# Seven block products for eight in the dense layers of an attention and gated-layer kernel, with the gated values passed through DRAM

## The chip, the cores and the metric

The kernel runs on one core of a Trainium2 chip. The metric is the device time of one execution in microseconds; a time is the median of several runs. The engines are TensorE (PE, with its weight loads shown apart as PEld), VectorE (DVE), ScalarE (ACT), GpSimd (POOL) and SyncE (SP), which here only issues DMAs.

## The reference

Random-feature attention on 8 batches, 8 heads, 576 tokens and a head size of 64 with 128 features, and behind it a gated layer on all 4608 tokens:

```python
def phi(x):
    proj = np.einsum('bhsd,md->bhsm', x, omega)
    sq = np.sum(x * x, axis=-1, keepdims=True) / 2.0
    h = proj - sq
    h = h - np.max(h, axis=-1, keepdims=True)
    return np.exp(h) / np.sqrt(m)
q_p, k_p = (phi(q_s), phi(k_s))
kv = np.einsum('bhsm,bhsd->bhmd', k_p, v)
z = np.sum(k_p, axis=2)
num = np.einsum('bhsm,bhmd->bhsd', q_p, kv)
den = np.einsum('bhsm,bhm->bhs', q_p, z)[..., None] + 1e-06
x = (num / den)                          # then to [4608 tokens, 512 columns]
gate = 1.0 / (1.0 + np.exp(-(x @ w_gate)))   # w_gate, w_val: 512 x 1536
val = x @ w_val
out = gate * val @ w_out                     # w_out: 1536 x 512
```

`q_s` and `k_s` are q and k scaled by 64 to the power of -1/4.

## The kernel before

**Precision.** A dense product is made in three passes of the array: each operand is split into a high part (`xh`, a rounded copy on ScalarE) and a low part (`xl`, the difference, on DVE or POOL), by `split` (L54, L55), and the passes wl·xh, wh·xl and wh·xh add up in PSUM. The weights of the dense layers come as float64 and are turned to float32 by `from_float64`, seven steps of integer arithmetic on DVE (L67 to L84) and one addition on POOL (L86) for each piece of 384 columns.

**Attention** is a list of tasks: norms of the rows, keys (features `kpk`, then the sums `kv`), queries (features, transposes to and fro, the division). Every task is a generator that yields after each step, and `attention` takes a step of each of up to six active tasks in turn. Its results go as `xT` to DRAM. A query step's chain on DVE is: largest projection `mxq` (L328), `hmq` (L331), `subq` (L389), the subtraction `hq` (L391); then PE transposes it, ScalarE takes the exponential, PE multiplies by `kv` to `pnq` (L414), DVE divides (`denq` L419, `invq` L423, `xq` L425) and PE transposes back (`pxq`, L431).

**The gated layers** take 12 column tiles of 128 of the 1536 columns, in two passes over all tokens (`passes`). The first pass takes tiles 0 to 3 with chunks of 256 tokens, two tiles in a bank, and writes its sums to the DRAM tensor `part`; the second takes tiles 4 to 11 with chunks of 512 tokens and adds `part` (L226). For a tile, `gated` makes the gate product (L178, bank `gv`), a sigmoid (L204), the value product, the gated product y (L207, DVE), its split (`yh` on ScalarE, `yl` on DVE), and a step later the output product (L192) into `acc` banks. The eight PSUM banks are divided as 4 `at` for attention and the sums, 2 `gv`, 2 `acc`.

**The order.** The main loop draws one piece of the gated layers, then RATE = 8 steps of attention, and every PUT = 5 pieces a piece of weight conversion; the converted weights of tiles 4 to 11 lie in the DRAM tensor `w32` until attention is through, when `late_weights` loads and splits them. That is the order of the program; a list scheduler then sets each engine's own order from it, and each engine works in order.

```python
while not ready(B * S):
    next(gates)
    credit += RATE
    while credit >= 1 and not ready(B * S):
        next(steps, None)
        credit -= 1
    n += 1
    if n % PUT == 0:
        next(conv, None)
```

## Time and profile before

| | |
|---|---|
| median of 3 runs | 1293.47 us (1292.13 to 1294.63) |
| span of the profiled execution | 1296.1 us, 2.6 over that median |
| PE busy | 1240.6 us, 96%, 7328 matmuls |
| DVE busy | 620.0 us, 48%, 1445 instructions |
| ACT busy | 520.4 us, 40%, 1119 instructions |
| POOL busy | 276.3 us, 21%, 304 instructions |
| mean granted clock of TensorE | 0.980 |
| DMA | 138.12 MB; HBM read 102.24 MB, written 34.60 MB |

The profile is of one execution. A busy time is a sum of lengths of instructions, and an instruction's length can hold time in which it waited for something that isn't shown. A page slices the span into 40 equal parts and gives each engine's busy share of a slice in tenths. A row of groups gives line, engine, operation, `out<-in` by the program's names, the count, busy time, the mean of one in ns, and the idle time just before these instructions with what ended it. A row of the timeline gives start, length, engine, line and operation, and in brackets how long the engine had been idle and what released it.

### The profile page before, as it was taken

How to read it: one execution, taken by the hardware profiler on the slowest of the kernel's cores; microseconds unless marked ns; L12 is line 12 of the kernel's file. 1: busy time of each engine (PE TensorE's matmuls, PEld its weight loads, DVE VectorE, ACT ScalarE, POOL GpSimd, SP SyncE). 2: the span in 40 equal slices, each digit the busy share in tenths (PEclk: the TensorE clock that was granted, in tenths of full speed). 3: DMA queues.
4: the chain of work that ended last, by engine and by line, in shares of the span. 5: the costliest groups of instructions: out<-in, count | busy, mean ns of one | idle time of the engine just before them, and what ended most of it. 6: DMA issues, size and time to landing. Idle time of an engine off the chain costs nothing.

```text
span 1296.1 us, 19491 instructions
## 1 busy us (share of the span) xinstructions
PE 1240.6 (96%) x7328; PEld 1077.6 (83%) x7328; DVE 620.0 (48%) x1445; ACT 520.4 (40%) x1119; POOL 276.3 (21%) x304
## 2 busy tenths in 40 slices
...
DVE  6989899998988574634111121212121212121212
...
PEclk8779999999999999999999999999999999999999
...
GB/s 272 203 178 139 183 228 242 186 241 212 221 174 171 103 119 52 50 178 140 51 49 81 1 98 1 98 1 98 1 98 1 98 1 98 1 98 1 60 6 33
DMA packets 76414, 138.12 MB, mean 107 GB/s; under 512 B 8480, under 2 KB 24096, under 8 KB 76320
## 3 DMA queue, kind: packets, MB, share of 16 engines
...
q14 instruction: 36, 0.29, 0.1%
HBM read 102.24 MB, written 34.60 MB: 106 GB/s over the span
## 4 chain that ended last, share of the span: by engine, by line
PE 73%; DVE 16%; issue 5%; DMA 4%; ACT 2%; POOL 0%; SPq 0%; DVEq 0%; POOLq 0%; ACTq 0%
PE gv L178 41%; PE acc L192 18%; PE pnq L414 4%; PE pkv L371 4%; PE ptq L402 2%; DVE mxq L328 2%; DMA w<-w 2%; DVE yl L55 1%; DVE hq L391 1%; DVE mxk L328 1%; DVE f64t L78 1%; DMA wraw<-w 1%; DVE subq L389 1%; DVE hmq L331 1%; DVE f64a L84 1%
## 5 line engine op out<-in xcount | busy, mean ns | idle before, releaser
L178 PE MATMUL gv<-xh,wl 128*128 128x256 f32 (+1 forms) x1152 | 394.7, 343 | 1.7 <-POOL wl L55 1.3
L178 PE MATMUL gv<-xl,wh 128*128 128x256 f32 (+1 forms) x1152 | 394.1, 342 | 0.8 <-POOL xl L55 0.8
L178 PE MATMUL gv<-xh,wh 128*128 128x256 f32 (+1 forms) x1152 | 393.4, 342 | 0.0
L207 DVE TENSOR_TENSOR y<-gv,y 128x512 f32<-128x512 f32 x108 | 74.6, 690 | 490.6 <-PE gv L178 439.1
L178 PEld LDWEIGHTS gv<-xh,wl 128*128 128x128 f32 x1152 | 219.4, 191 | 29.8 <-POOL wl L55 1.7
L178 PEld LDWEIGHTS gv<-xl,wh 128*128 128x128 f32 x1152 | 219.3, 190 | 27.9 <-POOL xl L55 1.0
L178 PEld LDWEIGHTS gv<-xh,wh 128*128 128x128 f32 x1152 | 219.3, 190 | 26.7
L55 POOL TENSOR_TENSOR xl<-xr,xh 128x512 fp32r<-128x512 f32 (+1 forms) x76 | 95.6, 1273 | 643.4 <-ACT xh L54 607.4
L192 PE MATMUL acc<-wh,yl 128*128 128x512 f32 x432 | 174.3, 403 | 5.3 <-DVE yl L55 4.9
L204 ACT ACTIVATE y<-gv 128x512 f32<-128x512 f32 x108 | 64.6, 598 | 283.0 <-PE gv L178 262.9
L192 PE MATMUL acc<-wl,yh 128*128 128x512 f32 x432 | 172.7, 400 | 0.0
L192 PE MATMUL acc<-wh,yh 128*128 128x512 f32 x432 | 171.5, 397 | 0.0
L54 ACT ACTIVATE yh<-y 128x512 fp32r<-128x512 f32 x108 | 68.2, 631 | 229.3 <-DVE y L207 228.7
L55 DVE TENSOR_TENSOR yl<-y,yh 128x512 fp32r<-128x512 f32 x108 | 85.2, 789 | 58.9 <-ACT yh L54 58.9
L192 PEld LDWEIGHTS acc<-wh,yl 128*128 128x128 f32 x432 | 81.4, 188 | 27.4 <-DVE yl L55 10.4
L192 PEld LDWEIGHTS acc<-wh,yh 128*128 128x128 f32 x432 | 81.6, 189 | 18.0
L192 PEld LDWEIGHTS acc<-wl,yh 128*128 128x128 f32 x432 | 81.6, 189 | 16.5
L55 POOL TENSOR_TENSOR loq<-rawq,hiq 128x256 fp32r<-128x256 f32 (+1 forms) x80 | 59.4, 753 | 118.5 <-ACT hiq L54 118.4
L363 ACT ACTIVATE kpk<-ppk,nbk 128x128 f32<-128x128 f32 x256 | 72.9, 376 | 25.2 <-DVE nbk L352 22.9
L371 PE MATMUL pkv<-v,kpk 128*128 128x66 f32 x512 | 77.5, 288 | 4.5 <-ACT kpk L363 4.2
L371 PEld LDWEIGHTS pkv<-v,kpk 128*128 128x128 f32 x512 | 71.1, 206 | 8.0 <-ACT kpk L363 7.2
L414 PE MATMUL pnq<-kv,qpq 128*128 128x66 f32 (+1 forms) x640 | 75.8, 272 | 0.2 <-ACT qpq L404 0.2
...
## 6 DMA issues: line engine op xcount, KB each, us to landing
...
xr<-xT SPq DMA_DIRECT2D x68, 256.0 KB, 4.0
...
natk<-kn SPq DMA_DIRECT2D x36, 256.0 KB, 4.4
natq<-qn SPq DMA_DIRECT2D x36, 256.0 KB, 3.7
part<-o ACTq DMA_DIRECT2D x36, 256.0 KB, 2.5
o<-part SPq DMA_DIRECT2D x36, 256.0 KB, 3.5
out<-o ACTq DMA_DIRECT2D x36, 256.0 KB, 3.8
```

Of the source, the lines that this page charges most:

```text
L54: nc.scalar.activation(out=hi, in_=x, func=AF.Copy)
L55: (lo_engine or nc.vector).tensor_tensor(out=lo, in0=x, in1=hi.bitcast(F32), op=ALU.subtract)
L78: nc.vector.scalar_tensor_tensor(out=t, in0=hi, scalar=0xC0000000, in1=t, op0=ALU.bitwise_and, op1=ALU.bitwise_or)
L178: nc.tensor.matmul(gv[:, g * C : (g + 1) * C], lhsT=a[:, o : o + P], rhs=x[k], start=(m == 0), stop=(m == 3 * KC - 1),)
L192: nc.tensor.matmul(acc[t], lhsT=a[:, s], rhs=b[:, o : o + DM], start=(j == js[0] and m == 0), stop=(j == js[-1] and m == 2),)
L204: nc.scalar.activation(out=y, in_=gate, func=AF.Sigmoid)
L207: nc.vector.tensor_tensor(out=y, in0=val, in1=y, op=ALU.mult)
L328: nc.vector.tensor_reduce(out=mx, in_=pp, axis=AX.X, op=ALU.max)
L363: nc.scalar.activation(out=kp[t][:, h, :], in_=pp[:, 2 * i + h, :], func=AF.Exp, bias=nb[:, i, h : h + 1], scale=SCALE,)
L371: nc.tensor.matmul(pkv[:, h, :], lhsT=kp[b * MID + i][:, h, :], rhs=v[:, i, h, :], start=(i == 0), stop=(i == MID),)
L402: nc.tensor.transpose(out=pt[:, i, :], in_=h_sb[:, i, :], identity=id_sb)
L414: nc.tensor.matmul(pn[r, 2 * i + h, :], lhsT=qp[:, 2 * i + h, r], rhs=kvs[u, p, bb][:, h, :], start=True, stop=True,)
```

## The change

**Blocks.** A 2x2 block product is formed from seven products instead of eight (Winograd's form of Strassen's scheme): with sums of blocks of both operands made ahead, and sums of the products behind. For gate and value the operands are blocks of 256 rows of x by 256 tokens and of 256 rows of the weights by 128 columns; a chunk is 512 tokens, a pair is 256 of the 1536 columns, and a product is 6 matmuls of 256 columns (2 row tiles, 3 passes). `PRODUCT` tells which operand of x and of the weights a product takes.

**Three stages.** Pairs 0 and 1 are taken for all nine chunks beside attention, pairs 2 to 5 for all chunks after it; both stages end at y, which is written to the DRAM tensor `yd`, so that `part` and the `acc` banks are gone. A third stage, `projected_out`, reads `yd` back in runs of 128 tokens, makes the block sums (L314), splits seven operands (`yh` on ScalarE, `yl` on DVE for three and on POOL for four), multiplies (L324, banks `po`) and makes the last sums (L332): 18 half chunks by three steps of two pairs.

**Work on the other engines.** Each kind (gate or value) of a pair and chunk has five sums on DVE (L210) and one copy on ScalarE; the first quarter of y is multiplied on DVE (L223), the other three on POOL (L235), in one instruction of 768 columns. Four sums of x's blocks for a chunk are made on DVE (L257), and seven operands instead of four are split with their low parts on POOL. The weights' block sums (L159) come ahead of their split. Weights are converted in 72 pieces of 256 columns instead of 48 of 384. One buffer holds g, two hold y; attention has 4 banks, the products 4.

**Attention.** The scale is folded into omega, so that L331, L352, L389 and L391 become plain two-operand instructions (L415, L437, L475, L477 now); raw tiles are fetched for each group instead of each task, and some pools have fewer buffers. RATE is 7, PUT 2, EVERY (first weights) 8.

The core of the diff; lines of the old functions that fall away are those printed above:

```diff
+PRODUCT = {1: (0, 0), 2: (1, 1), 3: (6, 2), 4: (2, 6), 5: (3, 3), 6: (4, 4), 7: (5, 5)}
...
+    yd = dram.tile([NPAIR, P, NCH, 4, Q], F32, name="yd")
...
+    banks = {"at": 4, "gv": 4}
...
+    def operands_of_weights(pool, temps, n, b, lo_engine):
...
+        t = temps.tile([P, 4, Q], F32, tag="g", bufs=1, name=f"wt{n}")
+        for o, x, y, op in (
+            (t[:, 0], b[:, 3], b[:, 0], ALU.subtract),
+            (t[:, 2], b[:, 2], b[:, 3], ALU.subtract),
+            (t[:, 1], b[:, 2], t[:, 0], ALU.subtract),
+            (t[:, 3], b[:, 1], t[:, 1], ALU.subtract),
+        ):
+            nc.vector.tensor_tensor(out=o, in0=x, in1=y, op=op)
+        split(nc, wh[:, :3], wl[:, :3], b[:, :3], lo_engine)
+        split(nc, wh[:, 3:], wl[:, 3:], t, lo_engine)
...
+    def late_weights(pools, temps, ns):
+        for n in ns:
+            b = temps.tile([P, 4, Q], F32, tag="y", bufs=2, name=f"wb{n}")
+            nc.sync.dma_start(out=b, in_=w32[n].rearrange("p (b q) -> p b q", q=Q))
+            operands_of_weights(pools[n], temps, n, b, nc.vector)
+            yield
+    def gated(pool, c, x, pair):
+        g = pool.tile([P, 4, Q], F32, tag="g", bufs=1, name=f"g{pair}_{c}")
+        y = pool.tile([P, 4, Q], F32, tag="y", bufs=2, name=f"y{pair}_{c}")
+        for kind, to in enumerate((g, y)):
+            id_ = f"{kind}_{pair}_{c}"
+            wh, wl = units[2 * pair + kind]
+            b0, b1, b2 = (any_bank(f"gv{i}_{id_}", "gv")[:, :Q] for i in range(3))
+            def product(n, o, first):
+                i, k = PRODUCT[n]
+                xh, xl = x[i]
                 m = 0
+                for kc in range(2):
+                    s = slice(kc * P, (kc + 1) * P)
+                    for u, v in ((wl, xh), (wh, xl), (wh, xh)):
                         nc.tensor.matmul(
+                            o, lhsT=u[:, k, s], rhs=v[:, kc, :], start=(first and m == 0), stop=(m == 5),
+                            skip_group_check=not first,
                         )
                         m += 1
+            def add(o, a, b):
+                nc.vector.tensor_tensor(out=o, in0=a, in1=b, op=ALU.add)
+            p1, u2, u3 = (
+                pool.tile([P, Q], F32, tag=t, bufs=2, name=f"{t}{id_}") for t in ("p1", "u2", "u3")
+            )
+            product(1, b0, True)
+            nc.scalar.activation(out=p1, in_=b0, func=AF.Copy)
+            product(6, b1, True)
+            add(u2, b1, p1)
+            product(5, b2, True)
+            yield
+            product(2, b0, False)
+            if kind:
+                nc.vector.tensor_tensor(out=y[:, 0], in0=b0, in1=g[:, 0], op=ALU.mult)
+            else:
+                nc.scalar.activation(out=g[:, 0], in_=b0, func=AF.Sigmoid)
+            product(7, b1, False)
+            add(u3, b1, p1)
+            add(to[:, 3], b2, u3)
+            yield
+            product(4, b1, False)
+            add(to[:, 2], b1, p1)
+            product(3, b2, False)
+            add(to[:, 1], b2, u2)
+            if kind:
+                nc.gpsimd.tensor_tensor(out=y[:, 1:], in0=y[:, 1:], in1=g[:, 1:], op=ALU.mult)
+                nc.scalar.dma_start(out=yd[pair, :, c], in_=y)
+            else:
+                nc.scalar.activation(out=g[:, 1:], in_=g[:, 1:], func=AF.Sigmoid)
+            yield
+    def load(pool, i, c):
+        raw = pool.tile([P, KC, NC], F32, tag="xr", bufs=1, name=f"xr{i}_{c}")
+        o = c * NC
+        while not ready(o + NC):
+            next(steps, None)
+        for k in range(KC):
+            nc.sync.dma_start(out=raw[:, k], in_=xT[k, :, o : o + NC])
+        x = {}
+        def put(n, a):
+            x[n] = [pool.tile([P, 2, Q], F32R, tag=t, bufs=XOPS, name=f"{t}{i}_{c}_{n}") for t in ("xh", "xl")]
+            split(nc, *x[n], a, lo_engine=nc.gpsimd)
+        def combined(n, a, b, op):
+            s = pool.tile([P, 2, Q], F32, tag="s", bufs=3, name=f"s{i}_{c}_{n}")
+            nc.vector.tensor_tensor(out=s, in0=a, in1=b, op=op)
+            return s
+        a11, a12, a21, a22 = raw[:, :2, :Q], raw[:, 2:, :Q], raw[:, :2, Q:], raw[:, 2:, Q:]
+        yield x
+        put(0, a11)
+        s1 = combined(3, a21, a22, ALU.add)
+        s2 = combined(4, s1, a11, ALU.subtract)
+        put(4, s2)
+        yield x
+        put(3, s1)
+        put(1, a12)
+        yield x
+        put(5, combined(5, a11, a21, ALU.subtract))
+        put(2, a22)
+        put(6, combined(6, a12, s2, ALU.subtract))
+        yield x
...
+    def projected_out(pool, c, s):
+        id_ = f"{c}_{s}"
+        po = [any_bank(f"po{i}_{id_}") for i in range(4)]
+        at = {n: po[i][:, h * Q : (h + 1) * Q] for i, ns in enumerate(((1, 2), (6, 7), (5, 3), (4,))) for h, n in enumerate(ns)}
+        for j in range(0, NPAIR, G):
+            raw = pool.tile([P, G, 4, P], F32, tag="yr", bufs=3, name=f"yr{id_}_{j}")
+            for g in range(G):
+                nc.sync.dma_start(out=raw[:, g], in_=yd[j + g, :, c, :, s * P : (s + 1) * P])
+            t = pool.tile([P, G, 4, P], F32, tag="ys", bufs=2, name=f"ys{id_}_{j}")
+            for o, a, b, op in (
+                (t[:, :, 0], raw[:, :, 2], raw[:, :, 3], ALU.add),
+                (t[:, :, 1], t[:, :, 0], raw[:, :, 0], ALU.subtract),
+                (t[:, :, 2], raw[:, :, 0], raw[:, :, 2], ALU.subtract),
+                (t[:, :, 3], raw[:, :, 1], t[:, :, 1], ALU.subtract),
+            ):
+                nc.vector.tensor_tensor(out=o, in0=a, in1=b, op=op)
+            yh, yl = (pool.tile([P, G, N_OPS, P], F32R, tag=g, bufs=5, name=f"{g}{id_}_{j}") for g in ("yh", "yl"))
+            split(nc, yh[:, :, 0:2], yl[:, :, 0:2], raw[:, :, 0:2], nc.vector)
+            split(nc, yh[:, :, 2], yl[:, :, 2], raw[:, :, 3], nc.vector)
+            split(nc, yh[:, :, 3:], yl[:, :, 3:], t, nc.gpsimd)
+            for g in range(G):
+                wh, wl = units[2 * NPAIR + j + g]
+                for n, o in at.items():
+                    i, k = PRODUCT[n]
+                    for m, (u, v) in enumerate(((yl, wh), (yh, wl), (yh, wh))):
                         nc.tensor.matmul(
+                            o, lhsT=u[:, g, i, :], rhs=v[:, k, :],
+                            start=(j + g + m == 0 and n in (1, 6, 5, 4)), stop=(j + g == NPAIR - 1 and m == 2),
+                            skip_group_check=True,
                         )
+            yield
+        def add(o, a, b):
+            nc.vector.tensor_tensor(out=o, in0=a, in1=b, op=ALU.add)
+        p1, u2, u3, u4 = (pool.tile([P, Q], F32, tag=f"o{t}", bufs=2, name=f"{t}o{id_}") for t in ("p1", "u2", "u3", "u4"))
+        o1, o2 = (pool.tile([P, 2, Q], F32, tag="o", bufs=4, name=f"o{i}_{id_}") for i in range(2))
+        nc.scalar.activation(out=p1, in_=at[1], func=AF.Copy)
+        add(u2, at[6], p1)
+        add(o1[:, 0], at[2], p1)
+        add(u3, at[7], u2)
+        add(o2[:, 1], at[5], u3)
+        add(u4, at[5], u2)
+        add(o1[:, 1], at[3], u4)
+        add(o2[:, 0], at[4], u3)
+        for o, r in ((o1, c * NC + s * P), (o2, c * NC + Q + s * P)):
+            nc.scalar.dma_start(out=out[r : r + P, :], in_=o)
...
+            conv = convert_weights(pool, units_of(LATE) + [2 * NPAIR + p for p in range(NPAIR)])
+            n = credit = 0
+            while not ready(B * S):
+                next(gates)
+                credit += RATE
+                while credit >= 1 and not ready(B * S):
+                    next(steps, None)
+                    credit -= 1
+                n += 1
+                if n % PUT == 0:
+                    next(conv, None)
+            for _ in conv:
+                pass
+        late = tail.enter_context(tc.tile_pool(name="late", bufs=1, side="right"))
...
+        cycle[:] = ["at", "gv"]
         n = 0
+        for _ in range(4):
+            next(conv)
+        for i, c, pair in gates:
+            if i and not c:
                 next(conv, None)
+            if i == 1 and c == NCH - 1:
+                n += 1
+                if n in (7, 9, 13, 14):
+                    next(last)
+    with tail:
+        with tc.tile_pool(name="out", bufs=1) as pool:
+            for c in range(NCH):
+                for h in range(Q // P):
+                    for k, _ in enumerate(projected_out(pool, c, h)):
+                        if not (c or h or k):
+                            for _ in last:
+                                pass
```

**DVE in attention's stretch.** The order of DVE before, at the queries' tile 4 of head pairs 0 to 2; `y` and `yl` are the gated layers' 512-wide product and low part, `f64` the weight conversion, the rest attention:

```order
L70 TENSOR_SCALAR f64a_1_7001<-f64a_1_7001 128x384
L207 TENSOR_TENSOR y_0_3411<-gv_0_1_3463,y_0_3411 128x512
L75 TENSOR_SCALAR f64t_1_7004<-f64a_1_7001 128x384
L419 TENSOR_SCALAR denq_0_4_3498<-pnq_0_4_3493 128x2
L78 SCALAR_TENSOR_TENSOR f64t_1_7004<-wraw_1_6999,f64t_1_7004 128x384
L423 RECIPROCAL invq_0_4_3500<-denq_0_4_3498 128x2
L328 TENSOR_REDUCE mxq_2_4_3508<-ppq_2_4_3504 128x2
L425 TENSOR_TENSOR xq_0_4_3502<-pnq_0_4_3493,invq_0_4_3500 128x128
L331 SCALAR_TENSOR_TENSOR hmq_2_4_3510<-mxq_2_4_3508,sqq_1_3347 128x2
L419 TENSOR_SCALAR denq_1_4_3525<-pnq_1_4_3520 128x2
L55 TENSOR_TENSOR yl_0_3490<-y_0_3411,yh_0_3489 128x512
```

At such a place now, again tile 4 of the queries, pairs 2 and 3; `u` and `g` at L210 are sums of products out of PSUM banks `gv`:

```order
L412 TENSOR_REDUCE mxq_3_4_3722<-ppq_3_4_3718 128x2
L503 TENSOR_SCALAR denq_2_4_3791<-pnq_2_4_3786 128x2
L415 TENSOR_TENSOR hmq_3_4_3724<-mxq_3_4_3722,sqq_1_3470 128x2
L210 TENSOR_TENSOR u_0_2_3765<-gv_0_0_2_3761,p_0_2_3763 128x256
L475 TENSOR_TENSOR subq_3_4_3726<-hmq_3_4_3724,sqq_1_3470 128x2
L507 RECIPROCAL invq_2_4_3793<-denq_2_4_3791 128x2
L210 TENSOR_TENSOR g_2_3758<-gv_0_0_2_3762,u_0_2_3765 128x256
L477 TENSOR_TENSOR hq_3_4_3728<-ppq_3_4_3718,subq_3_4_3726 128x256
L509 TENSOR_TENSOR xq_2_4_3795<-pnq_2_4_3786,invq_2_4_3793 128x128
L210 TENSOR_TENSOR g_2_3758<-gv_0_0_2_3761,p_0_2_3763 128x256
```

Between attention's small steps stand sums of 256 columns that read PSUM, and the low parts of y are gone from here.

**PE after attention.** Before, at the end of an output product in the second pass, the gate product of the tile after next stands behind it:

```order
L192 MATMUL acc_4_3_11662<-wh_9057,yl_9_11906 128x512
L192 MATMUL acc_4_3_11662<-wl_9058,yh_9_11905 128x512
L192 MATMUL acc_4_3_11662<-wh_9057,yh_9_11905 128x512
L178 MATMUL gv_11_0_11979<-xh_5_0_11566,wl_9314 128x512
L178 MATMUL gv_11_0_11979<-xl_5_0_11570,wh_9313 128x512
L178 MATMUL gv_11_0_11979<-xh_5_0_11566,wh_9313 128x512
```

Now, in the same stretch, the last matmul of product 7 (operand 5 of x) into bank `gv_1_3`, five matmuls of the next unit, and the first of product 4 (operand 2) into the bank of product 7:

```order
L203 MATMUL gv_1_3_5_12415<-xh_5_5_12170,wh_9100 128x256
L203 MATMUL gv_0_4_5_12473<-xh_5_0_12118,wl_9715 128x256
L203 MATMUL gv_0_4_5_12473<-xl_5_0_12119,wh_9714 128x256
L203 MATMUL gv_0_4_5_12473<-xh_5_0_12118,wh_9714 128x256
L203 MATMUL gv_0_4_5_12473<-xh_5_0_12118,wl_9715 128x256
L203 MATMUL gv_0_4_5_12473<-xl_5_0_12119,wh_9714 128x256
L203 MATMUL gv_1_3_5_12415<-xh_5_2_12174,wl_9101 128x256
```

Product 4 adds to that bank once DVE's sum `u3` has read it, so that the five matmuls between are the cover of that sum.

**DVE in the output stage.** In the new third stage, at the end of a half chunk (`ys` block sums of y, `po` banks of products, `o` results, `yl` low parts):

```order
L314 TENSOR_TENSOR ys_0_4_15185<-yr_0_4_15182 128x2x128 x2
L314 TENSOR_TENSOR ys_0_4_15185<-ys_0_4_15185,yr_0_4_15182 128x2x128
L332 TENSOR_TENSOR o_1_0_14856<-po_1_0_14674,p1o_0_14852 128x256
L332 TENSOR_TENSOR u2o_0_14853<-po_1_0_14675,p1o_0_14852 128x256
L314 TENSOR_TENSOR ys_0_4_15185<-yr_0_4_15182,ys_0_4_15185 128x2x128
L332 TENSOR_TENSOR u3o_0_14854<-po_1_0_14675,u2o_0_14853 128x256
L332 TENSOR_TENSOR o_1_0_14857<-po_1_0_14676,u3o_0_14854 128x256
L332 TENSOR_TENSOR u4o_0_14855<-po_1_0_14676,u2o_0_14853 128x256
L332 TENSOR_TENSOR o_1_0_14857<-po_1_0_14677,u3o_0_14854 128x256
L332 TENSOR_TENSOR o_1_0_14856<-po_1_0_14676,u4o_0_14855 128x256
L65 TENSOR_TENSOR yl_0_2_15133<-yr_0_2_15124,yh_0_2_15132 128x2x256
L65 TENSOR_TENSOR yl_0_2_15133<-yr_0_2_15124,yh_0_2_15132 128x2x128
```

Before, DVE's order at the end of a chunk, where the partial sums are added:

```order
L55 TENSOR_TENSOR yl_11_12410<-y_11_12393,yh_11_12409 128x512
L226 TENSOR_TENSOR o_4_0_12445<-acc_4_0_12060,o_4_0_12445 128x512
L226 TENSOR_TENSOR o_4_1_12449<-acc_4_1_12061,o_4_1_12449 128x512
L226 TENSOR_TENSOR o_4_2_12453<-acc_4_2_12062,o_4_2_12453 128x512
L226 TENSOR_TENSOR o_4_3_12457<-acc_4_3_12063,o_4_3_12457 128x512
L207 TENSOR_TENSOR y_4_12478<-gv_4_1_12480,y_4_12478 128x512
```

The last sums of a half chunk now stand in one run ahead of the low parts that the next products wait for.

333 lines of the change are left out of this document (128 added, 205 removed).

## The prediction

> **What bounds the kernel now.** I read the page first, then the busy time by stretches, the last attention instruction, the spacing of matmuls, and VectorE's (DVE's) instructions one by one.
>
> ```profile
> span 1296.1 us, 19491 instructions
> DVE  6989899998988574634111121212121212121212
> PEclk8779999999999999999999999999999999999999
> ...
> core 0: us, PE busy (x) PEld busy (x) DVE busy (x) ACT busy (x) POOL busy (x), PEclk, DMA share, GB/s
> 0.00:100.00 100.00, 72.48 (x424) 69.09 (x425) 82.44 (x208) 57.22 (x162) 52.49 (x67) 0.78 0.68 215
> 100.00:300.00 200.00, 189.90 (x1529) 177.97 (x1528) 186.60 (x514) 139.50 (x323) 85.33 (x98) 1.00 0.66 204
> 300.00:400.00 100.00, 94.11 (x727) 86.83 (x726) 86.66 (x236) 66.73 (x158) 39.26 (x45) 0.98 0.63 200
> 400.00:554.00 154.00, 151.10 (x1215) 141.92 (x1214) 95.18 (x266) 99.29 (x227) 37.12 (x48) 1.00 0.29 92
> 554.00:1296.00 742.00, 732.95 (x3442) 601.82 (x3440) 169.15 (x224) 157.71 (x252) 62.06 (x47) 1.00 0.17 56
> L431 PE MATMUL pxq<-id_sb,xq x144: 270/273/421, 53.6 to 552.9; 128*128 128x128 f32 x144
> ```
>
> There are two kernels in one. Up to 554 us attention runs (its last transpose, L431, starts at 552.9); DVE is 93% busy from 100 to 300 us (186.60 of 200) and TensorE (PE) 95%. After 554 us DVE needs 169 of 742 us and PE 733: that part is PE alone. So a change that takes work from PE and gives it to DVE gains behind 554 us and pays ahead of it.
>
> **Matmul time.** The spacing of matmuls, not their shown length, is their price.
>
> ```profile
> 599.73 0.28 PE L178 MATMUL gv<-xh,wl 128*128 128x256 f32 x1
> ...
> 606.45 0.28 PE L178 MATMUL gv<-xh,wh 128*128 128x256 f32 x1
> ...
> 904.74 0.40 PE L192 MATMUL acc<-wh,yl 128*128 128x512 f32 x1
> ...
> 907.31 0.39 PE L192 MATMUL acc<-wh,yh 128*128 128x512 f32 x1
> ...
> 1291.85 0.39 PE L192 MATMUL acc<-wh,yh 128*128 128x512 f32 x1
> ```
>
> 56 steps from 599.73 to 606.45 are 0.120 us each, 11 steps from 904.74 to 907.31 are 0.234. The dense layers were 1728 products of 256 columns and 3024 of 512: 207 + 707 = 914 us. Now they are 4536 for gate and value (9 chunks x 6 pairs x 2 x 7 x 6) and 2268 for the output (18 x 6 x 7 x 3), all of 256: 817 us. The saving is 97 us, not the 114 that one eighth of 914 would be, since two matmuls of 256 cost 0.240 for 0.234. In PE's order 1200 of the 4536 stand ahead of attention's last instruction (before: 1056 of the narrow ones and 251 of the 1296 of L192). Behind it stay 3336 x 0.120 = 400.3 us and 2268 x 0.120 = 272.2. For the old kernel this way of adding gives 554 + 672 x 0.120 + 2773 x 0.234 + 4.2 (from 1291.85 to the end) = 1288 us; the 8 us that lack are its waits.
>
> **Attention's stretch, by DVE.** Between independent neighbours DVE's spacing is shorter than the length shown:
>
> ```profile
> 223.00 0.68 DVE L288 TENSOR_REDUCE ssk<-x2k 128x8 f32<-128x512 f32 x1
> 223.59 0.17 DVE L423 RECIPROCAL invq<-denq 128x4 f32<-128x4 f32 x1
> ...
> 223.96 0.41 DVE L425 TENSOR_TENSOR xq<-pnq,invq 128x256 f32<-128x256 f32 x1
> 224.29 0.17 DVE L423 RECIPROCAL invq<-denq 128x4 f32<-128x4 f32 x1
> ...
> 227.51 0.55 DVE L78 SCALAR_TENSOR_TENSOR f64t<-wraw,f64t 128x384 uint32<-128x384 uint32 x1
> 227.97 0.15 DVE L331 SCALAR_TENSOR_TENSOR hmk<-mxk,sqk 128x4 f32<-128x4 f32 x1
> ...
> 229.44 0.35 DVE L82 TENSOR_SCALAR f64a<-f64t 128x384 uint32<-128x384 uint32 x1
> 229.70 0.15 DVE L352 SCALAR_TENSOR_TENSOR nbk<-sqk,hmk 128x4 f32<-128x4 f32 x1
> ```
>
> So 512 columns take 0.60 us, 256 take 0.33, a two-operand conversion step of 384 takes 0.46 and a one-operand step 0.26. Up to 554 us DVE was busy 82.4 + 186.6 + 86.7 + 95.2 = 450.9 us. Ahead of attention's last DVE instruction the new order has:
> - no gated products and low parts of 512: -44 x 0.60 = -26.4;
> - 140 sums of products (L210) and 14 gated products (L223) of 256: 154 x 0.34 = +52.4, and 28 sums that wait on the one just ahead of them, 0.1 each: +2.8;
> - 32 sums of x's blocks (L257) of 512, +19.2; 16 of the weights' blocks (L159), +5.4;
> - conversion of the weights in 72 pieces of 256 for 48 of 384. By the spacings a piece was 2 x 0.46 + 4 x 0.26 = 1.96; cut by 128 columns (0.13 and 0.06 a step) it is 1.46: 105 for 94, +11;
> - more waiting for GpSimd (POOL), next.
>
> ```profile
> L331 DVE SCALAR_TENSOR_TENSOR hmq<-mxq,sqq x80: 145/158/972, 39.9 to 547.5; 128x4 f32<-128x4 f32 x64, 128x2 f32<-128x2 f32 x16
> L331 DVE SCALAR_TENSOR_TENSOR hmq<-mxq,sqq 128x4 f32<-128x4 f32 x64 | 19.6, 311 | 0.2
> L391 DVE SCALAR_TENSOR_TENSOR hq<-ppq,subq x80: 406/675/692, 41.9 to 547.9; 128x512 f32<-128x512 f32 x64, 128x256 f32<-128x256 f32 x16
> 230.48 1.13 POOL L86 TENSOR_TENSOR f64t<-f64t,f64a 128x384 f32<-128x384 f32 x1 [1.25 <-DVE nbk L352]
> 230.78 1.05 DVE L70 TENSOR_SCALAR f64a<-f64a 128x384 f32<-128x384 f32 x1
> 700.00:800.00 100.00, 99.72 (x426) 79.89 (x425) 20.21 (x28) 16.70 (x27) 5.09 (x4) 1.00 0.10 32
> ```
>
> An instruction of four columns (L331) has a median of 158 ns, a mean of 311 and a longest of 972; one that reads PSUM (L391) never stretches (675 of at most 692). L70 at 230.78 takes 1.05 us and ends just after the POOL instruction that began ahead of it. So DVE instructions that work on SBUF alone wait out a running POOL instruction: about 0.14 us on each of the 320 small ones and 0.06 on 288 conversion steps, 62 us in all, while POOL was busy 214 us. POOL's work grows: 57 low parts of 512 for 29 smaller ones (+39 us, 1.27 each from the window's 5.09 for four), 14 gated products of 768 (+27, at the same rate 1.91 each), weights +3: 283 us. In proportion the waits grow by a third: +20 (0 if they hide, +60 if the longer POOL instructions block for all their length; I take proportion, as the rows are of the same operation).
>
> Sum: 450.9 + 84.4 = 535.3. The first 100 us (82.4 of it) stay; the rest needs 452.9 us of DVE at 95.5% busy, between 93.3% from 100 to 300 us and 100%, since PE has less to do there (at most 505 - 59 + 17 = 463 us): 474. Attention ends at 574 us, 20 later than now. ScalarE has 363 of 554 us; copies and sigmoids change it by some 20: no bound.
>
> **Behind it.** In the gated stage PE's product P4 adds to the bank of P7, so it waits for DVE's sum u3 of that bank. In 56 of 80 cases 5 matmuls of the next unit stand between: 0.60 us.
>
> ```profile
> 237.88 0.28 PE L325 MATMUL ppq<-omH,hiq 128*128 128x256 f32 x1
> 238.19 0.42 DVE L328 TENSOR_REDUCE mxq<-ppq 128x2 f32<-128x256 f32 x1 [0.84 <-PE ppq L325]
> 62.37 0.68 DVE L391 SCALAR_TENSOR_TENSOR hq<-ppq,subq 128x512 f32<-128x512 f32 x1
> 63.10 0.42 PEld L402 LDWEIGHTS ptq<-id_sb,hq 128*128 128x128 f32 x4 [0.62 <-DVE hq L391]
> xr<-xT SPq DMA_DIRECT2D x68, 256.0 KB, 4.0
> out<-o ACTq DMA_DIRECT2D x36, 256.0 KB, 3.8
> L54 ACT ACTIVATE wh<-w 128x768 fp32r<-128x768 f32 x16 | 13.5, 844 | 14.3 <-DMA w<-w 14.3
> ```
>
> From a matmul's slot end (237.88 + 0.12) to DVE 0.19, the sum 0.42, back to PE 0.05 (63.05 to 63.10): 0.66. Each is short by 0.06, or 0.2 when the weight load starts cold: 3 to 11 us, I take 8. At a change of chunk POOL makes the last low part (1.27), then the gated product of 768 (1.91); only then may DVE write g (one buffer), on which P3 hangs: about 4.5 us after the last P4, and PE has 29 matmuls (3.5 us) for it. With a p1 copy queued behind three x copies on ScalarE, 1.5 us for each of 10 changes: 15 (0 to 25). The late weights' 4 us of DVE per unit lie beside PE's products: 5 (0 to 10).
>
> The output stage cannot start before the last y is in DRAM: DVE 0.6, POOL 1.9, store 3.8, load 4.0 and its issue 0.4, four sums 1.7, copy of 1024 1.1, POOL 2.55, less 12 matmuls done meanwhile and with a cold clock after: 17 us (14 to 20). In it a step of 42 matmuls (5.04 us) needs four sums and two low parts on DVE (3 x 0.33 + 0.42 + 0.60 + 0.33 = 2.35) and 2.55 on POOL. One after the other they are 4.90 and fit; three steps also need 7 sums from PSUM, 2.7. If nothing overlaps, 17.4 for PE's 15.1, 18 times: 41 us; if the sums run under POOL, 0. The L391 row says that they can: I take 10. The loads of yd (108 of 256 KB, 28 MB in 272 us) stay under the 200 GB/s shown.
>
> 574 + 400.3 + 272.2 + 8 + 15 + 5 + 17 + 10 + 4.6 (the old tail and one short sum) = 1306 us of span. The profiled run was 2.6 us over the median of 1293.5, so 1304: 0.8% slower. The measurement tells no less than 0.2%.
>
> **Rivals.**
> 1. Faster: attention's stretch hardly grows, because the waits for POOL lie in time that DVE waited for PE anyway. DVE 515.3 at 97% ends it at 546; with 5 for the changes of chunk and no port loss that is 1258, 1256 by the median. It decides when attention ends before about 560. For: PE has 90 us to spare there. Against: DVE at 93% beside a PE that was also full. Chance 0.35.
> 2. The output stage is bound by DVE and POOL taking turns: +31 on the sum, 1335. It decides when a step takes over 5.3 us. The Trainium skill (SBUF — State Buffer, Who interferes with whom) says that a DVE instruction with two SBUF inputs is shut out for the whole of a GpSimd instruction that reads SBUF; by that rule every sum of y's blocks and low part queues with POOL's 2.55 us. The trace agrees for L70 and L331 above. Chance 0.12.
> 3. PE falls to half clock in attention's stretch, as in the first 100 us, where PE is 72% busy at a granted 0.78. At 463 of 574 us it would be 81% busy. 463 / 0.78 = 594 would then end the stretch, +20: 1324. The Trainium skill (TensorE: Matmul & The Clock Gate, Part 1) puts the half clock after an idle window of about 3.4 us; with matmuls waiting for single DVE sums such windows should be rare, and the row of 400 to 554 us shows 1.00. Chance 0.08.
>
> My forecast keeps 0.45. Below 1291 lie rival 1 and a little of the forecast, 0.36; within 0.2% 0.08; above 0.56. The range goes from rival 1's time to the sum with the upper ends of two or three terms (waits +40, stage end +31, less what excludes each other): 1258 to 1350. The forecast's own range is 1285 to 1330.
>
> **What would show it.** Attention's last transpose near 574 us with DVE over 93% busy to there; behind it 256-wide matmuls at 0.120 us with gaps of 0.1 to 0.2 ahead of every second P4; one PE gap of some 15 us ahead of the first po matmul; steps of 5.04 to 5.3 us after it. An end of attention before 560 makes me wrong on the sign; steps over 5.5 us, or gaps of a microsecond within a pair, make it slower than I say.

## The result and the profile after

The changed kernel takes 1423.65 us (median of 4 runs, 1420.94 to 1426.98) against 1292.82 for the kernel before: a ratio of 1.1005, with a 95% interval from 1.0978 to 1.1032. I had forecast 1304 and a range up to 1350; the sign was right, the size far off. The profiled execution spans 1423.5 us.

The first lines of the page, after the change:

```profile
span 1423.5 us, 26023 instructions
PE 1246.6 (88%) x9380; PEld 1193.6 (84%) x9380; DVE 1098.7 (77%) x2538; ACT 628.4 (44%) x1327; POOL 596.0 (42%) x478
DVE  7888898897987978877965544444548789999996
PEclk7666989897987988898999999999999799999999
HBM read 122.16 MB, written 54.53 MB: 124 GB/s over the span
```

PE is busy as long as before (1246.6 for 1240.6 us), although it has 97 us less to do at full clock. DVE, POOL and the clock row show where to look. By stretches, and with the row that dates attention's end:

```profile
0.00:100.00 100.00, 75.46 (x380) 72.05 (x381) 78.61 (x211) 50.08 (x135) 43.93 (x53) 0.68 0.57 175
100.00:300.00 200.00, 165.88 (x1257) 156.41 (x1255) 178.41 (x503) 124.69 (x289) 92.70 (x100) 0.87 0.52 155
300.00:400.00 100.00, 83.86 (x609) 79.54 (x609) 85.09 (x242) 60.47 (x132) 41.85 (x49) 0.90 0.57 169
400.00:554.00 154.00, 133.14 (x950) 125.44 (x949) 131.92 (x376) 95.25 (x221) 66.79 (x77) 0.86 0.56 172
554.00:646.00 92.00, 78.33 (x585) 73.68 (x586) 69.90 (x196) 49.33 (x111) 39.07 (x39) 0.89 0.33 102
646.00:750.00 104.00, 87.88 (x645) 84.02 (x645) 81.73 (x146) 41.16 (x69) 39.38 (x24) 0.92 0.32 113
750.00:1090.00 340.00, 319.42 (x2535) 306.91 (x2536) 173.25 (x377) 91.23 (x178) 124.97 (x83) 1.00 0.19 72
...
L515 PE MATMUL pxq<-id_sb,xq x144: 270/273/474, 57.0 to 646.2; 128*128 128x128 f32 x144
L324 PE MATMUL po<-wh,yl x756: 276/283/582, 1124.4 to 1418.1; 128*128 128x256 f32 x189
```

The columns are those of the same view before: stretch, its length, busy time of PE, PEld, DVE, ACT and POOL, granted clock, share of the DMA engines, GB/s. The last two rows give one line's instructions: count, shortest, median and longest length in ns, start of the first and of the last in us. Attention ends at 646 us instead of 553. To there no engine is full: PE 537 us busy of 646, DVE 544, with a granted clock of 0.68 and then 0.86 to 0.90 (before: 0.78, then 0.98 to 1.00). Of the 130 us, 93 are in attention's stretch. The other parts, each against the prediction's terms:

| part | predicted | measured |
|---|---|---|
| attention to its end | 574 | 646 |
| from there to the last gate or value product (1112.9) | 428 | 467 |
| gap ahead of the output stage | 17 | 11.5 |
| output stage (1124.4 to 1418.4) | 282 | 294 |
| tail | 4.6 | 5.1 |

### The profile page after: what moved, and what is told of

Read it like the earlier page. It is cut to its first block, busy times and chain, and to the rows that moved or that the text cites. A ratio compares the mean times of both kernels' runs of the same rounds, so it can differ in the third digit from the quotient of the medians.

```text
span 1423.5 us, 26023 instructions
## 1 busy us (share of the span) xinstructions
PE 1246.6 (88%) x9380; PEld 1193.6 (84%) x9380; DVE 1098.7 (77%) x2538; ACT 628.4 (44%) x1327; POOL 596.0 (42%) x478
## 3 DMA queue, kind: packets, MB, share of 16 engines
q10 hardware_dynamic: 29232, 58.08, 11.5%
## 5 line engine op out<-in xcount | busy, mean ns | idle before, releaser
L203 PE MATMUL gv<-xh,wl 128*128 128x256 f32 x1512 | 451.0, 300 | 54.5 <-DVE u L210 29.6
L203 PE MATMUL gv<-xl,wh 128*128 128x256 f32 x1512 | 437.1, 290 | 3.6 <-POOL xl L65 2.8
L203 PE MATMUL gv<-xh,wh 128*128 128x256 f32 x1512 | 424.4, 289 | 0.0
L324 PE MATMUL po<-wh,yl 128*128 128x256 f32 x756 | 217.8, 288 | 22.9 <-DVE yl L65 11.3
L324 PE MATMUL po<-wh,yh 128*128 128x256 f32 x756 | 214.3, 284 | 0.0
L324 PE MATMUL po<-wl,yh 128*128 128x256 f32 x756 | 214.1, 283 | 0.0
L235 POOL TENSOR_TENSOR y<-y,g 128x768 f32<-128x768 f32 x54 | 102.1, 1891 | 247.8 <-ACT p L216 125.5
L65 POOL TENSOR_TENSOR yl<-ys,yh 128x1024 fp32r<-128x1024 f32 x54 | 140.7, 2619 | 153.4 <-ACT yh L64 113.5
L324 PEld LDWEIGHTS po<-wh,yl 128*128 128x128 f32 x756 | 144.4, 191 | 29.1 <-issue 15.8
L210 DVE TENSOR_TENSOR u<-gv,p 128x256 f32<-128x256 f32 x216 | 89.5, 418 | 80.1 <-PE gv L203 77.1
L324 PEld LDWEIGHTS po<-wl,yh 128*128 128x128 f32 x756 | 144.5, 191 | 0.0
L324 PEld LDWEIGHTS po<-wh,yh 128*128 128x128 f32 x756 | 143.9, 190 | 0.0
```

The lines of the kernel that those rows point to most:

```text
L65: (lo_engine or nc.vector).tensor_tensor(out=lo, in0=x, in1=hi.bitcast(F32), op=ALU.subtract)
L203: nc.tensor.matmul(o, lhsT=u[:, k, s], rhs=v[:, kc, :], start=(first and m == 0), stop=(m == 5), skip_group_check=not first,)
L210: nc.vector.tensor_tensor(out=o, in0=a, in1=b, op=ALU.add)
L235: nc.gpsimd.tensor_tensor(out=y[:, 1:], in0=y[:, 1:], in1=g[:, 1:], op=ALU.mult)
L324: nc.tensor.matmul(o, lhsT=u[:, g, i, :], rhs=v[:, k, :], start=(j + g + m == 0 and n in (1, 6, 5, 4)), stop=(j + g == NPAIR - 1 and m == ...
```

## The experiments

Three questions: what lengthened attention's stretch (the first one), where the 39 us of the second stage went, and what the output stage costs. In the table, "end" is the start of attention's last transpose, "DVE" its busy time to there, "clock" the mean granted clock from 100 us to the end. Kernels whose first stage is the same code can get another order from the scheduler: the five with plain products ended attention at 554, 555, 555, 566 and 567 us, three with the first stage of the changed kernel at 640, 640 and 646. Differences below some 13 us are therefore not told apart, and each kernel's end is read from one trace.

| kernel | end | DVE | clock | span |
|---|---|---|---|---|
| before | 553 | 451 | 1.00 | 1296.1 |
| after | 646 | 544 | 0.88 | 1423.5 |
| e1_before_less | 551 | 450 | 0.95 | 1268.8 |
| e2_after_warm | 637 | 546 | 0.95 | 1432.2 |
| e3_plain_early | 566 | 452 | 0.95 | 1329.5 |
| e5_sums_act | 650 | 506 | 0.89 | 1427.5 |
| e7_before_dve | 593 | 516 | 0.95 | 1337.8 |
| e9_x_plain | 606 | 507 | 0.92 | 1376.7 |
| e10_no_sums | 647 | 501 | 0.88 | 1411.0 |
| e11_rate14 | 580 | 494 | 0.86 | 1425.0 |
| e13_x_seven | 624 | 523 | 0.90 | 1400.9 |
| e14_x_plain_no_sums | 616 | 469 | 0.90 | 1374.3 |
| e17_no_reads | 598 | 470 | 0.91 | 1359.3 |
| e18_warm_x_plain | 611 | 512 | 0.96 | 1400.0 |

**Is it the clock?** Two runs give PE less or more to do and leave the other engines alone.

```diff
 # e1_before_less (kernel before), first pass only
-for a, x in ((wl, xh), (wh, xl), (wh, xh)):
+for a, x in ((wl, xh), (wh, xl), (wh, xh))[1 if first else 0 :]:
 # e2_after_warm (changed kernel), behind every second matmul of pairs 0 and 1
+nc.tensor.matmul(spare[id(o)], lhsT=u[:, k, s], rhs=v[:, kc, :], start=False, stop=False,
+                 skip_group_check=True)
```

> The kernel before, with the pass wl*xh left out of the gate and value products of its first pass only: TensorE has 576 matmuls of 256 columns (69 us at 0.120) less to do beside attention, and VectorE, ScalarE and GpSimd have the same work as ever. Clock theory: with PE at some 80% instead of 95%, it falls to half clock in attention's stretch as in the changed kernel; half-clock time rises from 54 us to over 110 us, and attention's last transpose comes no earlier than 550 us, rather at 560 to 600, though there is less work. VectorE theory (sums and waits on DVE are what lengthened the stretch): nothing is added to DVE, so half-clock time stays below 80 us and the last transpose comes at 525 to 545 us.

> The changed kernel with idle matmuls: in the first stage's gate and value products every second matmul is made once more into the unused half of its bank, which nobody reads. That is some 585 matmuls, 70 us of PE at full clock, ahead of attention's end, so that PE's load there is as large as before the change. Clock theory: half-clock time falls from 235 us to under 150, and attention's last transpose comes no later than now (646 us), likely at 610 to 640, though there is more work. VectorE theory: PE only has more to do in front of attention's matmuls; the last transpose comes at 660 to 715 us.

With a third of its first pass's gate and value matmuls left out, the old kernel does fall to half clock more often (0.95 for 1.00 from 100 us on), but attention's end stays: 551 for 553. So PE's amount of work was not what held the old stretch. Neither theory fits whole: the VectorE theory had the end at 525 to 545; the clock theory had it at 550 or later, which held, but with over 110 us of half clock, and there were some 79 (worked out as below). With idle matmuls the changed kernel's clock rises:

```profile
0.00:100.00 100.00, 75.45 (x399) 71.37 (x399) 83.17 (x224) 53.54 (x147) 45.37 (x55) 0.73 0.57 179
100.00:637.00 537.00, 488.27 (x3932) 471.46 (x3931) 462.34 (x1297) 323.81 (x737) 230.09 (x256) 0.95 0.49 154
```

From these rows half clock lasts 2 x (27 + 0.05 x 537) = 108 us, and in the changed kernel 2 x (32 + 0.12 x 546) = 195. So 87 us of half clock went, and 70 us of matmuls came, and the end moved by 9. This is where the clock theory had put it (610 to 640), and not where the VectorE theory had (660 to 715). It shows that PE took 70 us of matmuls that wait for nothing new without a later end, so the amount of PE's work isn't the bound. It doesn't price the clock by itself: what a higher clock gave and what the added matmuls took can have cancelled.

**The first stage without the seven products; POOL's work behind attention on DVE.**

```diff
 # e3_plain_early: pairs 0 and 1
+for col in range(2):                      # one bank of 512 tokens for 128 columns
+    for kc in range(KC):
+        for u, v in ((wl, xh), (wh, xl), (wh, xh)):
+            nc.tensor.matmul(o, lhsT=u[:, k, s], rhs=v, start=(m == 0), stop=(m == 3 * KC - 1))
 # e4_low_dve
-nc.gpsimd.tensor_tensor(out=y[:, 1:], in0=y[:, 1:], in1=g[:, 1:], op=ALU.mult)
+(nc.gpsimd if pair in EARLY else nc.vector).tensor_tensor(
+    out=y[:, 1:], in0=y[:, 1:], in1=g[:, 1:], op=ALU.mult)
-split(nc, yh[:, :, 3:], yl[:, :, 3:], t, nc.gpsimd)
+split(nc, yh[:, :, 3:], yl[:, :, 3:], t, nc.vector)
```

> The changed kernel with the seven products undone in the first stage only: pairs 0 and 1 are made of plain products of 512 columns (708 of 0.234 us ahead of attention's end, 166 us, for 1200 of 0.120, 144 us), without sums on DVE, block sums of x or of the weights, p1 copies, or the gated product on GpSimd; later stages as they are. VectorE theory: DVE has some 90 us less to do ahead of attention's end and GpSimd some 50, so attention's last transpose comes at 550 to 580 us and the whole at 1330 to 1360. Clock theory: PE is still lighter than before the change (no output products there), half-clock time stays above 150 us and the last transpose comes after 600 us, the whole above 1375.

> The changed kernel with GpSimd's work behind attention moved to DVE: in the second stage the gated product of 768 columns, in the output stage the low parts of 1024. First stage as it is. Port theory (DVE instructions on SBUF wait for a running GpSimd instruction): in the output stage the sums L314 of 256 columns fall from 0.71 and 1.10 us to about 0.42 and DVE's busy time there from 275 us to below 250 though it has 54 longer instructions more; the stage falls from 294 us to 274 to 282. Theory that DVE's amount of work bounds it: DVE would need 275 + 54 x 1.2 = 340 us and the stage grows to over 320. Second stage (646 to 1113 us): if the chain through GpSimd at a change of chunk costs what was predicted (1.5 us and more for each of 9), it falls by 15 to 30 us; if one buffer for g alone is the cause, by under 10.

With plain products attention ends at 566 and the whole takes 1331.3 us: 80 of the 93 us come from the seven products and what they bring to the other engines. The VectorE theory's numbers held (550 to 580, 1330 to 1360), the clock theory's didn't (over 600, over 1375). The edit takes work from DVE, ScalarE and POOL at once, so it doesn't say which of them counts.

The output stage, first of the changed kernel, then of e4; in each, the rows of DVE are those from 1150 to 1390 us (line, operation, count, busy time, mean in ns, idle time before), and the last row is the whole stage:

```profile
L314 DVE TENSOR_TENSOR ys<-yr 128x256 f32<-128x256 f32 x92 | 60.8, 699 | 8.5 <-DMA yr<-yd 5.9 <-POOL yl L65 2.3
L314 DVE TENSOR_TENSOR ys<-ys,yr 128x256 f32<-128x256 f32 x46 | 49.9, 1086 | 0.0
1124.40:1418.40 294.00, 282.38 (x2268) 276.34 (x2268) 271.74 (x442) 106.18 (x178) 140.69 (x54) 0.99 0.41 124
```

```profile
L65 DVE TENSOR_TENSOR yl<-ys,yh 128x1024 fp32r<-128x1024 f32 x46 | 56.2, 1222 | 6.2 <-ACT yh L64 6.2
L316 DVE TENSOR_TENSOR ys<-yr 128x256 f32<-128x256 f32 x91 | 35.0, 421 | 1.2
1118.50:1395.00 276.50, 275.42 (x2268) 275.10 (x2268) 233.35 (x496) 109.24 (x178) 0.00 (x0) 0.99 0.43 132
```

DVE takes 54 instructions of 1.22 us more and is busy 38 us less: the first block sums fall from 0.70 to 0.42 us when POOL is still, and those of the second form from 1.09 to the same 0.42. The stage takes 276.5 us for PE's 2268 x 0.120 = 272. The whole gains 21.6 us (1402.0), 17.5 of them here. The other 4 are no more than the 6 us by which attention's end differs (640 for 646). In the second stage (640 to 1108 us, 468 long) the gated product's move gained nothing: the chain through POOL that I had priced there was not the one that mattered.

**The second stage's waits.** DVE's and PE's rows at a change of chunk in the changed kernel:

```profile
838.65 1.75 DVE L257 TENSOR_TENSOR s<-xr,s 128x512 f32<-128x512 f32 x1 [2.98 <-POOL xl L65]
840.32 0.74 DVE L210 TENSOR_TENSOR u<-gv,p 128x256 f32<-128x256 f32 x2
...
840.78 0.39 PE L203 MATMUL gv<-xh,wl 128*128 128x256 f32 x1 [1.61 <-DVE u L210]
847.70 0.36 PE L203 MATMUL gv<-xh,wl 128*128 128x256 f32 x1 [0.77 <-DVE g L210]
```

The fourth block sum of x needs the buffer (three for four) that POOL's low part still reads. It waits 3 us at the head of DVE's queue, the sum u that frees PE's bank stands behind it, and PE stands still. e6 gives the sums of the second stage six buffers:

```diff
-s = pool.tile([P, 2, Q], F32, tag="s", bufs=3, name=f"s{i}_{c}_{n}")
+s = (mid if i else pool).tile([P, 2, Q], F32, tag="s", bufs=6 if i else 3, name=f"s{i}_{c}_{n}")
```

> The changed kernel with six buffers instead of three for the block sums of x (L257) in the second stage alone, in a pool of its own. In the trace each change of chunk there has one L257 that waits 3 us for GpSimd's low part to release its buffer, with the sums u, for which PE waits 1.76 us, queued behind it on DVE. Buffer theory: that wait goes in eight changes, PE's gap of 1.76 with it and half of the 0.93 behind it, and the second stage (646 to 1113 us, 467 us long) gets 14 to 25 us shorter. Rival (GpSimd itself is late, since its low parts wait for x buffers that PE releases, and g waits for the gated product behind them): under 6 us shorter. Attention's end stays within 8 us of 646.

PE's waits from 750 to 1090 us before this edit, and with it (who waited <- for whom: us in total, times, longest):

```profile
PE gv L203 <- DVE u L210: 14.3, 9, 1.6
PE gv L203 <- DVE g L210: 6.1, 8, 0.8
```

```profile
PE gv L203 <- DVE g L210: 7.4, 8, 0.9
PE gv L203 <- DVE u L210: 5.5, 13, 1.4
```

The wait for u falls by 8.8 us as the buffer theory said, that for g stays. The stage is 457 us long for 467: between the two bounds that were written down (under 6, and 14 to 25), 10 of 39 us.

**Is it DVE's work?** e5 takes work from DVE in the first stage, e7 adds it to the old kernel.

```diff
 # e5_sums_act: pairs 0 and 1, the second addend left out
-nc.vector.tensor_tensor(out=o, in0=a, in1=b, op=ALU.add)
+nc.scalar.activation(out=o, in_=a, func=AF.Copy)
 # e7_before_dve: behind each maximum, twice
+nc.vector.tensor_reduce(out=spare, in_=om_sb.rearrange("p (i m) -> p i m", m=M), axis=AX.X, op=ALU.max)
```

> The changed kernel with the sums of products (L210) of the first stage made as plain copies on ScalarE, so that the second addend is left out: 140 instructions of 256 columns, 50 to 54 us, go from VectorE ahead of attention's end; PE, GpSimd and all else stay. In the runs so far attention's last transpose came 100 to 114 us of DVE idle time after DVE's busy time alone would have ended (451 + 102 before, 544 + 102 now). Theory that DVE's work adds to the stretch one to one: last transpose at 588 to 602 us, DVE idle there still 92 to 114. Clock and PE-wait theory: the products still gate PE, half-clock time stays above 150 us, and the last transpose comes after 620.

> The kernel before with two more VectorE instructions behind each maximum of projections: reductions of 256 columns of a constant into a scrap tile that nobody reads, 320 in all, some 100 us of DVE work spread over attention and nothing else changed. One to one theory: attention's last transpose moves from 553 to 640 to 660 us, with DVE idle time still near 100 us. What the prediction assumed (DVE's idle time ahead of attention's end is free for added work, up to 95.5% busy): last transpose at 570 to 590. Clock theory adds that half-clock time rises from 48 to over 100 us by that alone.

```profile
L518 PE MATMUL pxq<-id_sb,xq x144: 270/273/450, 56.7 to 649.9; 128*128 128x128 f32 x144
```

```profile
L436 PE MATMUL pxq<-id_sb,xq x144: 270/273/447, 56.7 to 592.6; 128*128 128x128 f32 x144
```

The first row is e5's: 38 us less DVE work, and the end stays (650); but ScalarE, which took the copies, is busy 415 us for 380. The second is e7's: 65 us more DVE work (100 had been expected) move the end by 40. The prediction's rule, 95.5% busy from 100 us on, would end e7 at 100 + 438.0 / 0.955 = 559 for the 593 measured. So the one to one theory, which had fitted the runs before, fell at once: DVE's idle time is neither free for added work, as the prediction had it, nor a constant. In e5 it grew from 102 to 144 us, where DVE now waited for PE's attention products.

**The x side or the sums.** e9 drops x's block sums and the three further operands that are split; e10 keeps those and drops everything behind the products (p1, u2, u3, the sums, POOL's gated product). e13 drops the block sums alone, e14 both sides. All in the first stage alone.

```diff
 # e9_x_plain: four blocks split, products 3 to 7 take one of them
+put(0, a11); put(3, a21); x[4], x[5] = x[0], x[3]
+put(1, a12)
+put(2, a22); x[6] = x[1]
 # e10_no_sums: each block straight from its bank
+to_sbuf(0, b0)      # gate: sigmoid on ScalarE; value: times g on DVE
 # e13_x_seven
+if i == 0:
+    return {3: a21, 4: a11, 5: a21, 6: a12}[n]     # instead of the sum
```

> The changed kernel with the block sums of x left out in the first stage: four blocks of x are split instead of seven operands, and the products that should take sums take one of the four. The products, their sums on DVE and the gated product on GpSimd stay. Ahead of attention's end that takes 32 instructions of 512 columns (32 us with their waits for GpSimd's reads) and 12 us of waits at the head of DVE's queue, some 24 low parts (31 us) from GpSimd and as many copies (15 us) from ScalarE. Theory that attention is a loop through all engines, in which any work queued ahead of its steps adds (the run with the sums moved from DVE to ScalarE gained nothing): last transpose at 600 to 622 us for 646. Theory that PE's products, which wait for DVE's sums, set it: above 636.

> The changed kernel with the sums behind the seven products left out in the first stage: no p1 copy, no u2, u3 and sums on DVE, no gated product on GpSimd; each of the four blocks goes straight from its bank through the sigmoid or the gated product of 256 columns. Block sums of x and of the weights stay, and PE has the same matmuls. Ahead of attention's end: some 35 us less on DVE, 27 on GpSimd, 15 on ScalarE, and no product waits for a sum. Loop theory: last transpose at 595 to 622 us. Theory of the x side (the head of DVE's and GpSimd's queues held by the splits of x): above 632.

> The changed kernel with the block sums of x (L257) alone left out in the first stage: seven operands are still split into their buffers (eight for seven), by ScalarE and GpSimd as before, but each takes a plain block of x. Leaving out the sums and the three further operands brought attention's last transpose from 646 to 606 us. If the sums at the head of DVE's queue are the cause: 603 to 614 us again. If it is the seven operands in eight buffers, whose copies and low parts fill ScalarE's and GpSimd's queues in a burst at each change of chunk: 630 to 646.

> The changed kernel with both left out in the first stage: the block sums and further operands of x, and the sums behind the products with GpSimd's gated product. PE makes the same 1200 matmuls ahead of attention's end. Alone, the first took 40 us from attention's stretch and the second none. If the second is hidden only as long as the first holds the queues: 566 to 580 us, as with plain products. If the sums cost nothing and the other 40 us come from the seven products' form on PE or from the weights' sums: 598 to 610.

Attention's last transpose in e9, e10, e13 and e14, in this order:

```profile
L526 PE MATMUL pxq<-id_sb,xq x144: 270/273/447, 56.1 to 605.8; 128*128 128x128 f32 x144
```

```profile
L539 PE MATMUL pxq<-id_sb,xq x144: 270/273/448, 56.3 to 647.1; 128*128 128x128 f32 x144
```

```profile
L517 PE MATMUL pxq<-id_sb,xq x144: 270/273/447, 55.6 to 623.6; 128*128 128x128 f32 x144
```

```profile
L550 PE MATMUL pxq<-id_sb,xq x144: 270/273/448, 55.8 to 616.0; 128*128 128x128 f32 x144
```

The x side is worth 40 us against 646, 34 against the two kernels of the same first stage that ended at 640: 16 to 22 for 32 block sums on DVE, 18 for 24 further copies and low parts on ScalarE and POOL, two halves of what e13 was to decide between. Each half is little more than a new order can do; the two together are clear of it. The 98 fewer sums and products of e10 on DVE (43 us of it, and 28 of POOL's) are worth nothing, with the x side (647) or without it (616, against e9's 606). One thing stands against calling these sums free: in e5, e10 and e14 ScalarE got 35, 21 and 26 us more to do in the same stretch (against the changed kernel, and e14 against e9), since it makes the copies or the sigmoids block by block, and no run takes the sums away without that. The sums behind the products were what I had priced highest, at 55 us; x's block sums I had at 19. What ScalarE, DVE and POOL wait for in the changed kernel between 114 and 646 us shows the difference:

```profile
ACT xh L64 <- DVE s L257: 15.4, 7, 5.4
ACT xh L64 <- PE gv L203: 12.1, 5, 6.1
POOL xl L65 <- ACT xh L64: 46.3, 20, 9.3
DVE s L257 <- POOL xl L65: 6.3, 5, 1.4
DVE s L257 <- DMA xr<-xT: 5.6, 4, 1.9
```

A sum behind a product waits for PE alone (4.1 us in seven waits for u), between attention's steps. A change of chunk is a ring of three engines: a sum on DVE, its copy on ScalarE, its low part on POOL, whose buffer the next sum needs, and a copy that waits for PE to be done with an operand (eight buffers for seven). Each of these waits stands at the head of an engine's queue, and attention's steps stand behind many of them: ScalarE's longest, 6.1 us at 272 us, has the exponential of a query step behind it, and one of 4.1 us on POOL at 390 us attention's own low parts. (The wait of 9.3 us comes at 645 us, when attention is through.) That these queues are how the 34 to 40 us come about is read from the rows; no run changes the order in the queues alone.

**How much of the dense work is hidden.**

```diff
-RATE = 7
+RATE = 14
```

> The changed kernel with 14 steps of attention for each piece of the gated layers instead of 7, so that about half as many dense matmuls (some 600 for 1200) stand ahead of attention's end and the rest behind it. If work beside attention were hidden, attention's end would move little (under 35 us) and the 600 matmuls would add 72 us behind: 1460 us or more. If it isn't hidden: the last transpose comes 70 to 100 us earlier, at 545 to 575 us, and the whole stays within 15 us of 1423. The weights are then converted in fewer steps before attention's end and partly behind it, which adds up to 20.

With 738 dense matmuls ahead of attention's end instead of 1200 it comes 66 us earlier, and the whole takes 1426.9 us, as before the edit: the 462 matmuls cost 0.14 us each in attention's stretch (66 / 462) and 0.15 behind it. So these 462 are not hidden in attention's stretch, with the sums and splits that come with them. The idle matmuls of e2 moved no end: PE's 109 idle us were open to matmuls that wait for nothing, and not to dense work that passes through the other engines.

**The rest of it.**

```diff
 # e17_no_reads: e14, and the bank of product 5 is read only after product 3
-to_sbuf(3, b2)
 yield
 product(4, b1, False)
 ...
+to_sbuf(3, b2)
 # e18_warm_x_plain: e9 with the idle matmuls of e2
```

> As the run without x's block sums and without the sums behind the products, but each bank of the first stage is read only after its last product, so that no product of a unit waits for a reader of its bank (a fourth block is taken from the bank that holds another). PE has the same 1200 matmuls of 256 columns and now runs a unit through, as with plain products. Coupling theory (PE, DVE and ScalarE wait for one another inside a unit): attention's last transpose falls from 616 us to 566 to 585. If the stretch keeps its length for the half clock that PE falls to with too little to do (167 us of it there): above 600, with half-clock time above 140.

> The run without x's block sums (last transpose at 606 us, 147 us of half clock to there), with every second dense matmul of the first stage made once more into the unused half of its bank: some 580 idle matmuls, 70 us at full clock, more work for PE. Clock theory: half-clock time falls below 95 us and the last transpose comes earlier, at 570 to 598, though there is more work. If PE's time isn't what holds it: 600 to 612. If PE's work bounds it: above 630.

```profile
L550 PE MATMUL pxq<-id_sb,xq x144: 270/272/447, 56.9 to 597.7; 128*128 128x128 f32 x144
```

e17 ends attention at 598 us, 18 earlier than e14: between the two theories' bounds (566 to 585, and over 600), and hardly more than a new order can do. e18 ends it at 611, with a clock of 0.96 for 0.92 and 70 us more of matmuls: not earlier than e9 (606), where the clock theory had 570 to 598. As in e2, more work and a higher clock came together. From e17 to plain products 32 to 44 us are left, over which I have no run: the two differ, among other things, in the width of the matmuls, in twelve more operands of the weights and their sums ahead of the first products, and in the banks that a unit holds (three for two). That stays open, and so does what a higher clock alone would give.

**A version put together.** Plain products in the first stage, DVE for the output stage's low parts, more buffers for x's block sums and for g in the second stage (e8); x loaded a pair earlier, with four buffers for x's block sums instead of six from here on (e12); two places for the loaded x (e15); the late weights' low parts on POOL besides (e16).

```diff
 # e8_best: e3, e4's second edit, e6, and in the second stage
+g = (pool if pair in EARLY else mid).tile(..., bufs=1 if pair in EARLY else 2)
 # e12_best2
-if pair == pairs[-1] and after:
+if pair == pairs[-2 if i else -1] and after:
 # e15_best3
+raw = (mid if i and c % 2 else pool).tile([P, KC, NC], F32, tag="xr", bufs=1, ...)
 # e16_best4
-operands_of_weights(pools[n], temps, n, b, nc.vector)
+operands_of_weights(pools[n], temps, n, b, nc.gpsimd)
```

> A version put together from the runs: plain products in the first stage, seven products in the second with six buffers for x's block sums and two for g, and the output stage's low parts all on DVE. By the parts: 1329.5 of the run with plain products, less 17 for the output stage, less 14 to 25 for the buffers of x's sums, less 0 to 8 for g: 1280 to 1299 us, so at or just under the kernel before (1293). If GpSimd's queue is what delays the second stage: 1305 to 1313.

> The version put together, with x of the second stage loaded one pair earlier (with four buffers for its block sums): in the trace of that version PE waits 1.2 to 1.6 us at each change of chunk for sums that stand on DVE behind a block sum that waits for that load. Eight such waits go: 8 to 13 us less than 1291.7, so 1278 to 1284. If DVE's queue is held by something else (the splits' buffers), no change within 3 us.

> The version put together (plain products in the first stage, low parts of the output stage on DVE, four buffers for x's block sums), with two places for the loaded x in the second stage by turns and two for g. In the version before, the load of x could be issued only when the last low part of the chunk ahead had read the one place, 4 us before it was needed, and PE lost 1.2 to 1.8 us for it at each of eight changes. If that is the cause: 8 to 13 us less, 1278 to 1284. If not: 1288 to 1294 as it was.

> The same with the low parts of the late weights on GpSimd instead of DVE (16 of 768 or 1024 columns for the second stage, 12 for the output weights). At the start of the second stage PE loses some 10 us to a copy and a sum that stand behind the weights' work on ScalarE and DVE. If DVE's load there is the cause: 3 to 8 us less than the version without. If GpSimd's longer instructions (2.6 us for 1024 columns) hold the weights up or stretch DVE's: 0 to 8 us more.

e8 takes 1291.7 us, a ratio of 0.9978 (0.996 to 0.9996) to the kernel before: 0.2% less, just clear of no difference, and that with the seven products only where PE is alone. No run takes the edits of attention itself alone, so how much of this is theirs isn't known. e12 is the same (1291.8, 0.9988, 0.9966 to 1.0009): the earlier load gained nothing; its transfers are still issued only when the low parts of the chunk ahead have read the one place for x. e15 (1315.2, 1.0162, 1.0123 to 1.0201) lost 1 to 2%, and e16 (1342.5, 1.0377, 1.0328 to 1.0426) 3 to 4%, of which 12 us may be order: its attention ended at 567 for 555. PE's wait for u in e15 from 575 to 1020 us doubled against e12 (30.5 us for 14.8). With the second place the block sums start earlier, and in DVE's rows they stand between the sums u, stretched by POOL or waiting for it:

```profile
697.66 2.29 DVE L282 TENSOR_TENSOR s<-xr,s 128x512 f32<-128x512 f32 x1 [0.43 <-POOL xl L65]
```

In e16 PE waited 27.5 us for the copy p1, 18.4 of them at once, behind the weights' copies on ScalarE:

```profile
PE gv L228 <- DVE u L235: 31.4, 16, 5.7
PE gv L228 <- ACT p L241: 27.5, 3, 18.4
```

In both, work that isn't urgent stands ahead of urgent work on an engine that takes its instructions in order.

## Why the prediction was wrong

- **What was right.** The price of a matmul (0.119 us apart at 800 us; I took 0.120), the count of work behind attention, DVE's work to attention's end (535 forecast, 544 measured), and that attention's stretch grows and makes the change slower. The gain behind it did not come: I had 732 us there for 743 before, and it took 777. The sign was right without it.
- **The step that failed: "the rest needs 452.9 us of DVE at 95.5% busy".** DVE's busy time came as forecast, but from 100 us on at 85% busy (465 of 546 us), so that attention lasted 646 us instead of 574: 72 of the 120 us by which I was low. I had read 93% busy from 100 to 300 us as a bound by DVE, and its 59 idle us from 400 to 554 as room. The runs show neither: with 65 us more on DVE the old kernel took 40 more, with 38 less the new one took as long. Of the 80 us that plain products win back, the x side, whose 19 us of sums and 39 us of POOL's low parts I had put under work and contention, makes 34 to 40; leaving out the sums behind the products, priced at 55 us of DVE, gained nothing measurable. The account that fits is a ring of engines that attention's steps pass through, in which added work costs by how it waits and not by its length. It is argued from the waits, and for the last 32 to 44 us the cause stays open.
- **Change of chunk, "1.5 us for each of 10 changes: 15".** I had looked for g behind POOL's product; of that PE's rows show 0.8 us. The longer wait was a block sum of x for its buffer, 1.6 us of PE's time, whose queue I had not followed. Buffers for it won 10 of the 39. The start of the stage took 104 us for 645 matmuls, 77 us' worth, where I gave 5 to the late weights: some 22 more. There PE waited 7.0 us for u, 4.4 for a copy of x and 3.4 for g, at a granted clock of 0.92; no run takes that part alone.
- **The output stage's contention, "I take 10".** The stage grew by 22 us over 272, and 17.5 went with POOL's low parts. Rival 2's mechanism was at work but not at its size: DVE was busy 272 of 294 us and PE still ran at 93%. The row that I took the 10 from (L391) reads PSUM, while the block sums read SBUF. The rule of the Trainium skill that it named (SBUF — State Buffer, Who interferes with whom) agrees: one form of the sums with two SBUF inputs took 1.09 us beside POOL and 0.42 without, while L332, which reads PSUM, kept 0.41. Of the two rows that I named for it, L331 has two such inputs, L70 only one.
- **Rival 3, half clock (chance 0.08).** It happened, with 195 us of half clock ahead of attention's end at PE 83% busy (I had estimated 81). What it cost isn't known: 87 us less of it, bought with 70 us of idle matmuls, gained 9, and in the second trial nothing. The way I had priced it, as PE's own time stretched by the clock, is not what the runs show, since the end doesn't follow PE's work.
- **Rival 1.** Its condition (the added waits lie in time that DVE waited for PE anyway) failed: attention ended 93 us later, though PE had 109 idle us.
